# Swapping the operands of the state read, moving its scaling behind the product, and a new list of pieces

## The chip, the cores and the metric

The kernel runs on one core of one Trainium2 chip. TensorE (PE) multiplies, VectorE (DVE), ScalarE (ACT) and GpSimd (POOL) do the elementwise work, and SyncE (SP), ACT and POOL issue DMAs. The metric is the time of one execution on the device in microseconds. Before the change the median of three runs is 211.62 us (211.5 to 211.73). The profiled execution took 211.45 us in all; its span, from the first to the last instruction, is 209.7 us, so 1.75 us lie around the span, and it stands 0.17 us below the median.

## The reference

Inputs are `x` (8 batches, 8 heads, 512 rows, 64 columns) and `state` (8, 8, 32, 64), in float32. Attention is done twice, once from `x` to `state` and once from `state` to `x`:

```
scores  = x @ state.T / 8 ;  a  = softmax(scores)  ; xread = a  @ state    # 512 rows a head
scores2 = state @ x.T / 8 ;  a2 = softmax(scores2) ; sread = a2 @ x        # 32 rows a head
y = concat([xread, sread]), heads side by side: (8 * 544, 512)
out = (s * relu(y @ w_in)**2 + b) @ w_out                                  # d_ff = 2048
```

The change concerns `sread`, the second attention, whose 8 * 8 * 32 rows are computed from the softmax over the 512 rows of `x`.

## The kernel before, in words

All work is cut into small pieces. Each piece is a Python function, and a list written out by hand, `ORDER` (L15), gives the sequence in which they are emitted. A word such as `l.3.5` or `S.2.1.0.V` is a piece, its numbers and, where it can run on several engines, the engine (`A`, `V` or `G` for ACT, DVE and POOL). Each engine, and each engine's DMA queue, works strictly in the order in which its own instructions stand in the list; between engines only data and buffers make one wait for another. The first number of a word is the batch as a rule.

For one batch `b` the pieces are these. `x` or `xn` loads the rows of x (POOL's queue), `xT` or `xt` transposes them (DVE for batches 0 to 2, a DMA transpose on SP's queue for 3 to 7). `T` computes the scores into two PSUM banks; `U`, `mu`, `D`, `E1`, `z`, `At`, `A` are the first softmax. `M` multiplies the states into `w_in` (PE) and `Mc` copies that to SBUF (ACT or DVE): for `xread` the reading of the state and the first layer are one product. `l` is a block of layer 1, two matmuls of 512 columns and a Relu on ACT, through a pool of two PSUM banks (`ps_h`); `lh` is its half for the start. `s` and `sh` square it. Layer 2 is `L` with `out` for batch 0, and for batches 1 to 7 a fast form with seven products, `P.b.0` to `P.b.13`, with sums of the operands before (`S`, DVE or POOL), `ev` behind (DVE, out of PSUM) and `put` (two stores each on SP's queue). `wsum` makes the sums of weights.

The second attention: `nm`, `nms` take the maximum, `E2` is the exponential on ACT (L425), one instruction for each group of four heads, which also adds up each row. `a2` (L433) divides: a reciprocal, then two DVE instructions of 128x512 that scale and reorder. `tr` (L446) transposes by DMA on SP's queue. `V` (L450) is the product: the 64 columns of one head of x are the loaded weights and 32 columns of the transposed softmax move through, 32 matmuls a batch. `srd` (L470) copies the result on ACT straight into `srdT`, in which the batches lie side by side in the innermost place, 16 bytes from one element to the next. When all eight batches are there, `lsr`, `ssr`, `S_sr`, `P_sr` and `ev_sr` put the 2048 rows of `sread` through both layers, among the products of batches 6 and 7. `idle` are matmuls without use at the start. `cs` copies transposed states within SBUF (four DMAs on SP's queue). PSUM has two pairs of banks for `T`, `M`, `V` and others (`own` chooses), two banks for `l`, two for the products.

Of the kernel before, what the change touches and what calls it, by code (L numbers as in the profile page):

```python
# [10 lines left out]
FP32 = mybir.dt.float32  # L11
FP16 = mybir.dt.float16
# [70 lines left out]
def kernel(  # L83
# [31 lines left out]
    XB = 3  # L115
    scale = float(1.0 / np.sqrt(D))
# [59 lines left out]
    srdT = konst.tile([P, NK, Ns, B], FP16, name="srdT")  # L176
# [145 lines left out]
    def at_T(b, own=1, p=None):  # L322

        if b >= XB:
            at[b]["T", None] = T = two_banks(f"T_{b}", own=own)
            for g in range(NG):
                for c in range(2):
                    rows = slice(D * c, D * c + D)
                    for hp in range(4):
                        r = hp ^ 2 * g  # L330
                        h = 4 * g + r
                        mm(
                            T[Ns * hp : Ns * hp + Ns, c, HALF * g : HALF * g + HALF],
                            stC[rows, b - XB, g, Ns * r : Ns * r + Ns],
                            at[b]["xT"][rows, 2 * h : 2 * h + 2],
                            tp=(D * c, Ns * hp),
                        )
            return
# [131 lines left out]
    def at_srd(b):  # L470
        nc.scalar.copy(srdT[:, :, :, b], at[b]["vps"])
# [347 lines left out]
```

## Time and profile before

| | before |
|---|---|
| median of 3 runs | 211.62 us |
| profiled execution, its own time | 211.45 us |
| its span | 209.7 us |
| mean granted TensorE clock | 0.984 |
| busy: PE, DVE, ACT, POOL | 200.1, 179.0, 169.1, 47.4 us |
| chain that ended last | PE 86%, DVE 6%, DMA 3% |
| HBM read and written | 20.48 MB, 8.91 MB |

The page's first part gives each engine's busy time; its second cuts the span into 40 slices of 5.24 us and gives the busy share of each in tenths. The chain of work that ended last goes back from the last instruction, at each step to what released it. The groups of instructions give the mean duration of one and what ended the idle time before it. A view by windows gives the busy time of each engine in any stretch.

### The profile page before, as it was taken

How to read it: one execution, taken by the hardware profiler on the slowest of the kernel's cores; microseconds unless marked ns; L12 is line 12 of the kernel's file. 1: busy time of each engine (PE TensorE's matmuls, PEld its weight loads, DVE VectorE, ACT ScalarE, POOL GpSimd, SP SyncE). 2: the span in 40 equal slices, each digit the busy share in tenths (PEclk: the TensorE clock that was granted, in tenths of full speed). 3: DMA queues.
4: the chain of work that ended last, by engine and by line, in shares of the span. 5: the costliest groups of instructions: out<-in, count | busy, mean ns of one | idle time of the engine just before them, and what ended most of it. 6: DMA issues, size and time to landing. Idle time of an engine off the chain costs nothing.

```text
span 209.7 us, 4807 instructions
## 1 busy us (share of the span) xinstructions
PE 200.1 (95%) x1939; PEld 131.4 (63%) x1939; DVE 179.0 (85%) x276; ACT 169.1 (81%) x275; POOL 47.4 (23%) x63
## 2 busy tenths in 40 slices
PE   7498998999999999999999999999999999999992
PEld 2134343344576757676677677766777677888881
DVE  2998999799999899999999999999995984476571
ACT  4589999999999999989999677997989688634500
POOL 8553360524074009300470007100000000000000
PEclk9859999999999999999999999999999999999999
DMA  6999999699448539959799353719004910440055
GB/s 152 179 207 207 195 205 204 110 144 165 99 79 96 107 78 183 147 86 195 163 128 189 74 118 65 100 42 199 12 0 88 187 31 0 96 107 0 5 149 152
DMA packets 42475, 24.87 MB, mean 119 GB/s; under 512 B 24532, under 2 KB 37588, under 8 KB 42452
## 3 DMA queue, kind: packets, MB, share of 16 engines
q0 software_dynamic: 15408, 9.90, 34.0%
q1 hardware_dynamic: 25760, 13.70, 31.3%
q10 hardware_dynamic: 1284, 0.95, 1.6%
q8 instruction: 15, 0.25, 0.5%
q14 instruction: 8, 0.07, 0.1%
HBM read 20.48 MB, written 8.91 MB: 140 GB/s over the span
## 4 chain that ended last, share of the span: by engine, by line
PE 86%; DVE 6%; DMA 3%; ACT 1%; POOL 1%; issue 1%; DVEq 0%; POOLq 0%
PE opf_X L142 24%; PE hps L509 23%; PE opf_W L142 12%; PE opf_Y L142 6%; PE ops L558 5%; PE mps L142 4%; DMA w_in<-in_moe_w_in_dram 3%; PE hps_sr L509 3%; PE vps L142 2%; PE ops_sr_X L142 2%; DVE M L157 1%; PE hph L142 1%; ACT M L157 1%; PE dps L733 1%; PE ops_sr_W L142 1%; DVE g L519 1%
## 5 line engine op out<-in xcount | busy, mean ns | idle before, releaser
L513 ACT ACTIVATE r<-hps 128x512 f16<-128x512 f32 x120 | 69.2, 619 | 11.1 <-PE hps L509 9.0
L142 PEld LDWEIGHTS <-g 128*128 128x128 f16 x672 | 65.2, 98 | 17.8 <-issue 1.5
L509 PE MATMUL hps<-A,M 128*128 128x512 f16 x240 | 64.8, 379 | 0.4 <-ACT M L157 0.3
L517 ACT ACTIVATE g<-r 128x1024 f16<-128x1024 f16 (+1 forms) x37 | 46.1, 1262 | 0.0
L509 PEld LDWEIGHTS <-M 128*128 128x128 f16 x240 | 22.0, 98 | 19.7 <-issue 5.2
L142 PE MATMUL opf_X<-w_T,g 128*128 128x256 f16 x224 | 28.4, 273 | 0.0
L634 DVE TENSOR_TENSOR g<-g 128x1024 f16<-128x1024 f16 (+1 forms) x36 | 25.5, 709 | 0.6
L157 ACT CAST M<-mps 128x1024 f16<-128x1024 f32 x21 | 21.2, 1032 | 2.5 <-PE mps L142 2.5
L196 POOL DMA_DIRECT2D xn<-in_x_dram x32 | 18.5, 584 | 4.2 <-DMA w_in<-in_moe_w_in_dram 1.8
L634 POOL TENSOR_TENSOR g<-g 128x1024 f16<-128x1024 f16 x4 | 8.5, 2125 | 46.1 <-DVE g L634 32.4
L664 DVE SCALAR_TENSOR_TENSOR osx<-opf_X,sb_bc,bias_bc 128x512 f32<-128x512 f32 x21 | 15.5, 737 | 1.5 <-PE opf_X L142 1.4
L558 PE MATMUL ops<-w_out,g 128*128 128x512 f16 x64 | 16.0, 379 | 0.0
L142 PE MATMUL opf_X<-w_out,g 128*128 128x256 f16 x112 | 14.4, 273 | 0.0
L142 PE MATMUL opf_Y<-w_out,g 128*128 128x256 f16 x112 | 14.3, 273 | 0.0
L142 PE MATMUL opf_W<-w_T,g 128*128 128x256 f16 x112 | 14.2, 273 | 0.0
L142 PE MATMUL opf_X<-w_T,S 128*128 128x256 f16 x112 | 14.2, 272 | 0.0
L142 PE MATMUL opf_W<-w_out,g 128*128 128x256 f16 x112 | 13.9, 273 | 0.0
L142 PE MATMUL mps<-w_in,stT 64*32 64x512 f16 x256 | 12.4, 411 | 1.4 <-DMA w_in<-in_moe_w_in_dram 1.4
L157 DVE CAST M<-mps 128x1024 f16<-128x1024 f32 x11 | 13.2, 1215 | 0.4 <-PE mps L142 0.4
L513 ACT ACTIVATE r_sr<-hps_sr 128x256 f16<-128x256 f32 x16 | 6.1, 382 | 9.2 <-PE hps_sr L509 8.5
L142 PEld LDWEIGHTS <-S 128*128 128x128 f16 x112 | 11.0, 98 | 2.9 <-issue 0.2
L634 DVE TENSOR_TENSOR S<-g 128x1024 f16<-128x1024 f16 x14 | 9.5, 682 | 2.3 <-ACT g L517 2.2
(98 smaller groups left out, 272.9 us busy)
## 6 DMA issues: line engine op xcount, KB each, us to landing
out_dram<-osx SPq DMA_DIRECT2D x52, 128.0 KB, 2.4
xn<-in_x_dram POOLq DMA_DIRECT2D x32, 128.0 KB, 5.3
w_in<-in_moe_w_in_dram POOLq DMA_DIRECT2D x8, 256.0 KB, 9.4
w_out<-in_moe_w_out_dram POOLq DMA_DIRECT2D x4, 512.0 KB, 13.2
xh<-in_x_dram POOLq DMA_DIRECT2D x4, 256.0 KB, 11.3
out_dram<-osb SPq DMA_DIRECT2D x16, 64.0 KB, 1.8
xf<-in_x_dram SPq DMA_DIRECT2D x2, 256.0 KB, 3.6
out_dram<-osx ACTq DMA_DIRECT2D x4, 128.0 KB, 2.9
```

Source lines behind the costliest of these rows:

```text
L142: return nc.tensor.matmul(out, lhsT, rhs, start=start, stop=stop, tile_position=tp, is_transpose=is_transpose, skip_group_check=skip,)
L157: (engine.copy if engine is nc.scalar else engine.tensor_copy)(out, in_)
L196: nc.gpsimd.dma_start(out=xn_t[b][32 * jh : 32 * jh + 32].rearrange("t h c d -> t h (c d)"), in_=x[b].rearrange("h (t jh c) d -> jh t h (c ...
L509: nc.tensor.matmul(to, lhsT, rhs, start=(i == 0), stop=(i == len(terms) - 1))
L513: nc.scalar.activation(R_t[tag, q][:, i], hps, AF.Relu)
L517: nc.scalar.activation(g, r, AF.Square)
L519: e.tensor_mul(g, r, r)
L558: nc.tensor.matmul(ops_t[tag, rr], G_t[tag][:, f, P * rr : P * rr + P], w_out_f(f), start=(v == 1 and f == 4 * q), stop=(v == NKF // 4 and ...
L634: e.tensor_tensor(out, x, y, op)
L664: nc.vector.scalar_tensor_tensor(out, fast(b, name[0]), s_bc, out if plus else bias, ALU.mult, ALU.add)
L733: nc.tensor.matmul(dps, ones16[:, :P], ones16, start=True, stop=True)
```

## The change

- `V` is turned round: 32 columns of the transposed exponentials are loaded as weights, and the 64 columns of x move. The result has the rows of the state in the partitions and the columns of four heads in the free dimension. There are 32 matmuls a batch as before, now over four groups of columns of the array rather than two. With `own` 2 its place in PSUM is a bank of layer 1's pool.
- The exponentials aren't divided before the product. `a2` is gone; `E2` writes its values in the order that `a2` had written (two buffers now, one before), `tr` transposes them, and only the reciprocal, `q`, is left of the division.
- `srd` scales the product by `q` on its way out of PSUM, on ACT: one instruction of 128x64 for each group of heads, or two of 64x64 where the heads are turned (group 1 of batches 0 to 2).
- `srt`, new, transposes that 128x128 block by DMA on SP's queue, one for each batch. `sro`, new, two pieces on ACT, each of 128x512, reads the eight blocks at a step of 256 bytes and writes what `lsr` reads.
- For batches 3 to 7 the heads of group 1 aren't turned any more in `T` and `M`.
- `ORDER` is new throughout. Beside the places, engines change: of eight elementwise pieces on POOL two stay (`At.3.G`, `S.1.2.0.G`); one goes to ACT (`s.0.8.2`) and five to DVE (`D.2`, `S.1.1.1`, `S.2.2.0`, `At.5`, `S.4.4.1`). Three casts `Mc` more on ACT and three fewer on DVE, five wide squares (`s.b.f.4`, 128x2048) from ACT to DVE and one back, `castx.1` and two `turn` on DVE. In the loads, `win.1` stands before `win.0`, and `win.3` and `st` before the first `wout`.

```diff
     def at_E2(b, g):
-        E2, rs = sm(b, "E2", [P, NG, S], FP16), sm(b, "rs", [P, NG], FP32)
+        E2, rs = sm(b, "E2", [P, NG, S], FP16, bufs=2), sm(b, "rs", [P, NG], FP32)
+        if b < XB:
+            to = E2[:, g].rearrange("p (c jh t) -> p jh c t", c=4, jh=4)
+            by = scores(b)[:, g].rearrange("p (jh c t) -> p jh c t", c=4, jh=4)
+        else:
+            to = E2[:, g].rearrange("p (k c q) -> p c k q", k=2, c=2)
+            by = of_head(b, scores(b), g).rearrange("p c (k q) -> p c k q", k=2)
         nc.scalar.activation(
-            E2[:, g] if b < XB else E2[:, g].rearrange("p (c q) -> p c q", c=2),
-            of_head(b, scores(b), g), AF.Exp,
+            to, by, AF.Exp,
...
-    def at_a2(b):
-        q, a2 = sm(b, "q", [P, NG], FP32), sm(b, "a2", [P, NG, S], FP16)
-        nc.vector.reciprocal(q, at[b]["rs"])
-        for g in range(NG):
...
-            nc.vector.tensor_scalar(to, by, q[:, g : g + 1], None, ALU.mult)
+    def at_q(b):
+        nc.vector.reciprocal(sm(b, "q", [P, NG], FP32, bufs=3), at[b]["rs"])
...
     def at_V(own, *bs):
...
-                    for g in range(NG):
-                        hp = k ^ 2 * g
+                    for hp in range(4):
                         mm(
-                            vps[D * g : D * g + D, k, :],
-                            xn[:, 4 * g + k, i, :],
-                            a2T[:, SCH * g + i, Ns * hp : Ns * hp + Ns],
+                            vps[Ns * hp : Ns * hp + Ns, D * g : D * g + D],
+                            E2T[:, SCH * g + i, Ns * hp : Ns * hp + Ns],
+                            xn[:, 4 * g + (hp ^ turned(b, g)), i, :],
...
-                            tp=(0, D * g),
+                            tp=(0, Ns * hp),
...
-    def at_srd(b):
-        nc.scalar.copy(srdT[:, :, :, b], at[b]["vps"])
+    def at_srd(b, e):
+        sr16 = sm(b, "sr16", [P, P], FP16, apool, SRB)
+        for g in range(NG):
+            cols, n = slice(D * g, D * g + D), P // 2 if turned(b, g) else P
+            for p in range(0, P, n):
...
+                    nc.scalar.activation(to, by, AF.Copy, scale=q)
...
+    def at_srt(b):
+        nc.sync.dma_start_transpose(out=srdT[:, b : b + 1, :], in_=at[b]["sr16"])
...
+    def order_sr(h, e):
...
+        ks = slice(2 * h, 2 * h + 2)
+        copy(e, by_slot[0][:, ks], srdT.rearrange("p b (k n) -> p k n b", n=Ns)[:, ks])
```

The list itself is too long to show; the stretches of the new one on which the prediction rests are these, word for word, and "..." stands for what lies between:

```
l.2.5 E2.3.1 ev.1.X1 L.0.3.1 D.3.V xt.4 L.0.3.2 l.2.7 l.2.10 E1.3 T.4.0 M.2.3.1 out.0.3 wsum.T2.1.V Mc.2.3.A
nm.4 nms.4.A E2.4.1 q.3 s.2.6.2.V l.2.3 P.1.2 z.3 E2.4.0 s.2.4.2.A P.1.3 At.3.G P.1.5 M.3.0.1 P.1.4 cs.6.8
ev.1.Y l.2.13 U.4 l.2.12 P.1.7 mu.4 P.1.6 Mc.3.0.A s.2.0.2.A l.2.9 tr.3 ev.1.X2 S.1.4.1.V V.0.3 srd.3.A
...
l.6.2 P.4.11 put.3.1.0 S.5.3.0.V put.3.1.1 ev.4.X3 l.5.14 l.6.3 Mc.6.3.A s.5.14.2.A P.4.12 s.5.12.2.V P.4.13
l.6.1 P.5.3 ev.4.W2 D.7.V srt.4 M.6.1.1 M.7.1.0 Mc.7.1.A ev.4.X4 E2.7.0 S.5.1.0.V l.6.0 tr.0 q.0 l.6.8
S.5.3.1.V P.5.1 P.5.0 put.4.0.1 put.4.0.0 P.5.2 Mc.6.1.V S.5.1.1.V srt.2 E2.7.1 nm.1 q.7 E1.7 l.6.10 tr.6
S.5.2.1.V ev.5.X1 M.7.2.0 put.4.1.0 V.1.6.0 ev.5.Y l.6.11 tr.7
...
P.5.12 l.7.3 ev.5.W2 Mc.7.3.A P.6.1 l.7.7 srd.1.A put.5.0.0 put.5.0.1 s.6.4.4.V l.7.0 S.6.3.0.V srt.5 S.6.1.0.V
S.6.2.1.V P.6.0 ev.5.X4 P.6.2 l.7.15 l.7.6 srt.1 s.7.6.2.A P.6.3 s.7.2.2.V s.7.4.2.A ev.6.X1 S.6.2.0.V srt.7
l.7.9 sro.1.A l.7.11 P.6.5 put.5.1.1 ev.6.Y P.6.4 P.6.6 sro.0.A l.7.13 P.6.7 S.6.4.0.V ev.6.X2 l.7.14 s.7.0.2.A
S.6.4.1.V lsr.6
```

More of the change, by code (lines that the diff above doesn't have):

```diff
@@ L115 @@
     XB = 3
+    SRB = 4
     scale = float(1.0 / np.sqrt(D))
@@ L175 @@
     bias_bc = konst.tile([P, DM], FP32, name="bias_bc")
-    srdT = konst.tile([P, NK, Ns, B], FP16, name="srdT")
+    srdT = konst.tile([P, B, P], FP16, name="srdT")
     w_in16 = [wpool.tile([P, NK, 512], FP16, name=f"w_in16_{j}") for j in range(NJ)]
@@ L328, in at_T @@
                     rows = slice(D * c, D * c + D)
-                    for hp in range(4):
-                        r = hp ^ 2 * g
-                        h = 4 * g + r
+                    for r in range(4):
+                        hp, h = r, 4 * g + r
                         mm(
@@ L427, in at_E2 @@
         nc.scalar.activation(
-            E2[:, g] if b < XB else E2[:, g].rearrange("p (c q) -> p c q", c=2),
-            of_head(b, scores(b), g), AF.Exp,
+            to, by, AF.Exp,
             bias=at[b]["nms"][:, g : g + 1], scale=scale, accum_out=rs[:, g : g + 1],
         )
-    def at_a2(b):
-        q, a2 = sm(b, "q", [P, NG], FP32), sm(b, "a2", [P, NG, S], FP16)
-        nc.vector.reciprocal(q, at[b]["rs"])
-        for g in range(NG):
-            to, by = a2[:, g], at[b]["E2"][:, g]
-            if b < XB:
-                to = to.rearrange("p (c jh t) -> p jh c t", c=4, jh=4)
-                by = by.rearrange("p (jh c t) -> p jh c t", c=4, jh=4)
-            else:
-                to = to.rearrange("p (k c q) -> p c k q", k=2, c=2)
-                by = by.rearrange("p (c k q) -> p c k q", k=2, c=2)
-            nc.vector.tensor_scalar(to, by, q[:, g : g + 1], None, ALU.mult)
+    def at_q(b):
+        nc.vector.reciprocal(sm(b, "q", [P, NG], FP32, bufs=3), at[b]["rs"])
@@ L446, in at_tr, with turned @@
     def at_tr(b):
-        a2T = sm(b, "a2T", [P, NG * SCH, P], FP16, apool, 2)
-        nc.sync.dma_start_transpose(out=a2T, in_=at[b]["a2"].rearrange("p g s -> p (g s)"))
+        E2T = sm(b, "E2T", [P, NG * SCH, P], FP16, apool, 2)
+        nc.sync.dma_start_transpose(out=E2T, in_=at[b]["E2"].rearrange("p g s -> p (g s)"))
+    def turned(b, g):
+        return 2 * g if b < XB else 0
     def at_V(own, *bs):
-        pair = two_banks(f"vps_{bs[0]}", own=own)
+        if own == 2:
+            place = ps_h.tile([P, 512], FP32, name=f"vps_{bs[0]}", tag="ph")
+        else:
+            place = two_banks(f"vps_{bs[0]}", own=own)[:, 0, :]
@@ L453, in at_V @@
         for v, b in enumerate(bs):
-            vps = pair[:, v, : NK * Ns].rearrange("p (k n) -> p k n", n=Ns)
-            a2T, xn = at[b]["a2T"], xn_t[b]
-            for k in range(NK):
+            vps = place[:, P * v : P * v + P]
+            E2T, xn = at[b]["E2T"], xn_t[b]
+            for g in range(NG):
                 for i in range(SCH):
-                    for g in range(NG):
-                        hp = k ^ 2 * g
-                        mm(
-                            vps[D * g : D * g + D, k, :],
-                            xn[:, 4 * g + k, i, :],
-                            a2T[:, SCH * g + i, Ns * hp : Ns * hp + Ns],
+                    for hp in range(4):
+                        mm(
+                            vps[Ns * hp : Ns * hp + Ns, D * g : D * g + D],
+                            E2T[:, SCH * g + i, Ns * hp : Ns * hp + Ns],
+                            xn[:, 4 * g + (hp ^ turned(b, g)), i, :],
@@ L464, in at_V @@
                             start=(i == 0),
                             stop=(i == SCH - 1),
-                            tp=(0, D * g),
+                            tp=(0, Ns * hp),
                         )
             at[b]["vps"] = vps
-    def at_srd(b):
-        nc.scalar.copy(srdT[:, :, :, b], at[b]["vps"])
+    def at_srd(b, e):
+        sr16 = sm(b, "sr16", [P, P], FP16, apool, SRB)
+        for g in range(NG):
+            cols, n = slice(D * g, D * g + D), P // 2 if turned(b, g) else P
+            for p in range(0, P, n):
+                to, by = sr16[P - n - p : P - p, cols], at[b]["vps"][p : p + n, cols]
+                q = at[b]["q"][p : p + n, g : g + 1]
+                if e is nc.scalar:
+                    nc.scalar.activation(to, by, AF.Copy, scale=q)
+                else:
+                    e.tensor_scalar(to, by, q, None, ALU.mult)
@@ L473, in at_M @@
+    def at_srt(b):
+        nc.sync.dma_start_transpose(out=srdT[:, b : b + 1, :], in_=at[b]["sr16"])
+    by_slot = []
+    def order_sr(h, e):
+        if not by_slot:
+            by_slot.append(konst.tile([P, 2, NK, Ns, B], FP16, name="srp", tag="Ts_2")[:, 0])
+        ks = slice(2 * h, 2 * h + 2)
+        copy(e, by_slot[0][:, ks], srdT.rearrange("p b (k n) -> p k n b", n=Ns)[:, ks])
     def at_M(b, j, own):
@@ L477, in at_M @@
             for g in range(NG):
-                r = hp ^ 2 * g
+                r = hp ^ turned(b, g)
                 mm(
@@ L507, in layer1 @@
         for i, (lhsT, rhs) in enumerate(terms):
-            to = hps if len(rhs.shape) == 2 else hps.rearrange("p (c q) -> p c q", c=2)
+            to = hps if len(rhs.shape) == 2 else hps.rearrange("p (c q) -> p c q", c=rhs.shape[1])
             nc.tensor.matmul(to, lhsT, rhs, start=(i == 0), stop=(i == len(terms) - 1))
@@ L544, in layer1_sr @@
     def layer1_sr(f):
-        layer1("sr", f, [(w_in_f(k, f), srdT[:, k].rearrange("p n b -> p (n b)")) for k in range(NK)], B * Ns)
+        layer1("sr", f, [(w_in_f(k, f), by_slot[0][:, k].rearrange("p n b -> p (n b)")) for k in range(NK)], B * Ns)
     ops_t, visits = {}, {}
@@ L777 @@
         "sb": spread_scalars, "xT": at_xT, "xt": at_xt, "cs": copy_states, "T": at_T, "keep": at_keep, "U": at_U, "mu": at_mu, "D": at_D,
-        "E1": at_E1, "z": at_z, "At": at_At, "A": at_A, "nm": at_nm, "nms": at_nms, "E2": at_E2, "a2": at_a2,
-        "tr": at_tr, "V": at_V, "srd": at_srd, "M": at_M, "Mc": at_Mc,
+        "E1": at_E1, "z": at_z, "At": at_At, "A": at_A, "nm": at_nm, "nms": at_nms, "E2": at_E2, "q": at_q,
+        "tr": at_tr, "V": at_V, "srd": at_srd, "srt": at_srt, "sro": order_sr, "M": at_M, "Mc": at_Mc,
         "lh": layer1_half, "sh": square_half, "l": layer1_x, "s": square, "lsr": layer1_sr,
```

127 rows, old and new, of the table ORDER are left out of this document.

## The prediction

> **What bounds the kernel now.** I read the page's busy times and slices first.
>
> ```profile
> PE 200.1 (95%) x1939; PEld 131.4 (63%) x1939; DVE 179.0 (85%) x276; ACT 169.1 (81%) x275; POOL 47.4 (23%) x63
> PE   7498998999999999999999999999999999999992
> DVE  2998999799999899999999999999995984476571
> PEclk9859999999999999999999999999999999999999
> ```
>
> A busy PE needn't be PE at its peak, so the chain that ended last comes next, in order of time; then windows over its parts (columns: PE, PEld, DVE, ACT, POOL busy).
>
> ```profile
> 19.62 1.25 DVE U L361
> ...
> 31.34 1.25 DVE xT L311
> 32.64 0.64 PE T_None L142 x16
> 33.49 0.54 PE hps L509 x2
> ...
> 38.57 0.86 PE ops L558 x4
> ...
> 73.52 0.56 PE mps L142 x16
> ...
> 75.97 0.87 PE opf_X L142 x8
> ...
> 204.77 0.89 PE ops_sr_X L142 x8
> ```
>
> ```profile
> 33.49:83.00 49.51, 49.51 (x445) 28.16 (x443) 47.19 (x66) 48.17 (x74) 16.53 (x17) 1.00 0.72 122
> 120.00:165.00 45.00, 45.00 (x449) 31.74 (x448) 41.47 (x66) 39.03 (x64) 4.38 (x5) 1.00 0.45 85
> 165.00:205.66 40.66, 40.65 (x407) 34.20 (x404) 26.52 (x45) 21.55 (x41) 0.00 (x0) 1.00 0.29 67
> ```
>
> From 33.49 to 205.66 us the chain is PE without a gap, at full granted clock, and at the full pace: four matmuls of 512 columns in 0.86. So an `l` is 0.43 of PE's time, a `P` (8 of 256) 0.87, an `M` (8 of the 16) 0.28. Ahead of 33.49 it runs through DVE: the last link is `xT.2`, for which `T.2.1` waits. So the time is (when `T.2.1` can start) + (PE's work behind it, 172.2) + (a tail that stays). Behind 33.49 a gain can come only from less PE work; a loss from anything that makes PE wait. DVE has 49.51 - 47.19 = 2.3 us of idle time up to 83 us, 3.5 from 120 to 165. It is the engine with the least to spare.
>
> **The change, part by part.** The sum goes against the profiled execution, 211.45 us in all, 0.17 below the median of 211.62.
>
> *The product `V`.* From the chain, and one row of the groups of tile vps:
>
> ```profile
> 36.62 0.98 PE cps L142 x16
> 47.43 0.34 PE T L142 x16
> 65.51 0.61 PE vps L142 x32
> 105.13 1.16 PE vps L142 x64
> ```
>
> Before: 0.61 + 0.61 for the two single batches and 1.16 or less for each pair, 4.6 us for eight, some 18 ns a matmul. After: 32 matmuls a batch again, of 32 weight columns and 64 moving ones, in four column groups. The floor is streaming: `cps`, four groups of full height, does 16 * 512 columns in 0.98, so 32 * 64 are a quarter, 0.24. The other end is today's pace, 18 ns a matmul, 0.58. `T` loads 32-column weights and takes 0.34 for 16, with twice the moving columns a group; 13 to 14 ns, a little under today's, is nearest in kind: 0.44 a batch. **V: -1.1 us** (0 to -2.7). It stands on the chain, so all of it counts.
>
> The Trainium skill, TensorE: Matmul & The Clock Gate, section "Wait — 56ns, not 53.3ns?", says that matmuls never start less than about 25 ns apart, however few columns move. By that, 32 take 0.80 us and V costs 1.8 us more than before instead of less. The trace speaks against it for products in column groups: 64 in 1.16 us are 18 ns each.
>
> *Scaling and copies off PE.*
>
> ```profile
> L444 DVE TENSOR_SCALAR a<-E,q 128x512 f16<-128x512 f16 x16 | 4.9, 350 | 0.3
> L471 ACT CAST srdT<-vps 128x128 f16<-128x128 f32 x8 | 5.9, 740 | 0.0
> L513 ACT ACTIVATE r<-hps 128x512 f16<-128x512 f32 x120 | 69.2, 619 | 11.1 <-PE hps L509 9.0 <-DVE g L519 1.4
> L513 ACT ACTIVATE r_sr<-hps_sr 128x256 f16<-128x256 f32 x16 | 6.1, 382 | 9.2 <-PE hps_sr L509 8.5 <-DVE g_sr L519 0.4
> L517 ACT ACTIVATE g<-rh 128x512 f16<-128x512 f16 x2 | 1.3, 630 | 0.0
> L157 DVE CAST M<-mps 128x1024 f16<-128x1024 f32 x11 | 13.2, 1215 | 0.4 <-PE mps L142 0.4
> L519 DVE TENSOR_TENSOR g<-r 128x2048 f16<-128x2048 f16 x2 | 2.4, 1218 | 0.5 <-ACT r L513 0.5
> L369 DVE TENSOR_TENSOR Dm<-U,mu 128x1024 f32<-128x1024 f32 x6 | 7.3, 1210 | 0.0
> L634 DVE TENSOR_TENSOR g<-g 128x1024 f16<-128x1024 f16 x34 | 23.1, 679 | 0.6
> ```
>
> DVE loses 16 scalings, 5.6 us. ACT's `srd` changes from 8 * 0.74 = 5.9 to 5 * 2 + 3 * 3 = 19 copies of 64 columns; from 0.382 and 0.619 for 256 and 512 columns a column is 0.93 ns, so 0.20 each, 3.9. `sro` adds two of 128x512: 0.63 each if a read at a step of 256 bytes costs nothing. If it costs what the scattered write of `srdT` costs (0.74 where 0.26 would do for 128, so 3.7 ns an element more), 2.5 each. I take 0.63: a read is not that write; 2.5 is kept for the range. `E2` writes runs of 32 or 128 values, and I cost its new order at nothing; ACT's spare time before `V` would cover it.
>
> The Trainium skill, SBUF — State Buffer, section "Door 1: The DMA port swizzle", says that SBUF has lines of 16 bytes and each access to a new line pays. By that `sro` is the slow case. The 0.74 of `srdT`, one element in each 16 bytes, agrees; no row here reads so.
>
> *DVE's load.* The new list gives back what `a2` freed. Up to `P.2.0` DVE loses 4 scalings (1.4), one cast (1.2), three squares and a wide one (2.0 + 1.2) and three halves `sh` (1.2), together 7.0; it gains `D.2` (1.2) and `S.1.1.1` (0.7) from POOL, two casts (2.4), two squares and three wide ones (1.4 + 3.7), `castx.1` and two `turn` (about 1.1, estimated from the copies), together 10.5: 3.5 us more, and 4.8 with two sums and an eviction that now stand ahead of `P.2.0`. Against that it no longer meets POOL's square at the start:
>
> ```profile
> L519 DVE TENSOR_TENSOR g<-rh x6: 382/404/1328, 16.4 to 29.4; 128x512 f16<-128x512 f16 x6
> 28.08 2.33 POOL L519 TENSOR_TENSOR g<-r 128x1024 f16<-128x1024 f16 x1
> 29.36 1.33 DVE L519 TENSOR_TENSOR g<-rh 128x512 f16<-128x512 f16 x1
> ```
>
> That half square took 1.33 where its like take 0.40, and ended just behind POOL's: 0.95 saved. Net +2.5 to +3.8 us, against 2.3 of idle time up to 83. Up to `T.2.1` I walked DVE's list with these durations: `U.1` at 18.8 (19.62 before), then `Mc.0.2`, `mu`, `D`, `Mc.0.3`, a square, `turn`, `z`, `At`, `A`, `pair`, `Mc.2.0`, a half square, `xT.2`, ending at 32.8 against 32.6, with PE's work ahead of `T.2.1` equal (20 us by the pieces). **Start: +0.2** (-1 to +1.5). Behind it DVE is nearly without idle time up to 83 us, and PE needs its sums and evictions: **+0.6** (0 to 2).
>
> *SP's queue.* The transposes of DMA are now the last link of three chains.
>
> ```profile
> 52.69 4.27 SPq L572 DMA_DIRECT2D out_dram<-osb  x8
> 58.57 2.59 SPq L275 DMA_DIRECT2D stC<-stT  x4
> 139.28 2.48 SPq L673 DMA_DIRECT2D out_dram<-osx  x4
> L448 SPq DMA_TRANSPOSE a2T<-a x8: 1236/1254/1360, 57.3 to 163.3; - x8
> a2T<-a SPq DMA_TRANSPOSE x8, 3.1
> L664 DVE SCALAR_TENSOR_TENSOR osx<-opf_W,sb_bc,osx 128x512 f32<-128x512 f32 x7 | 5.2, 746 | 2.3 <-PE opf_W L142 2.3
> ```
>
> `tr.3` now stands behind `out.0.3` (4 stores) and `cs.6.8` on SP, where before `cs.6.8` came after. From the start of `out.0.3`: 0.74 on DVE, 2.1 for its stores, 2.6 for `cs.6.8`, 3.1 to landing: 8.6 us. PE's work between these places is 4 `l`, 6 `P` and an `M`: 7.2. `V.0.3` waits up to 1.4, less if DVE takes `out.0.3` early, for which 1.4 us of PE's work leaves room. I take 0.6. `tr.6` stands behind `put.4.0.1`, `put.4.0.0` (four stores, which wait for `ev.4.W2`) and `srt.2`. From the start of `ev.4.W2`: 0.74 + 2.5 + `srt.2` (0 to 1.25; the trace has no transpose that small) + 3.1 = 6.3 to 7.6. PE's work to `V.1.6.0`: 3 `l`, 3 `P`, 3 `M`, 4.7. It waits up to 2.8; nothing if DVE is 2 to 3 us ahead of the list there, where it has idle time. I take 0.6. PE waits in order, so all that stands behind `V` waits too, and ACT's `E2.1` needs the buffer that `tr.6` reads. **SP: +1.2** (0 to 4.1).
>
> Of the eight `srt` six are early; the last two aren't. SP holds `put.5.0.0`, `put.5.0.1` ahead of them, which end some 1.9 us behind the start of `srd.1` (`ev.5.W2` starts one `P` and one `l`, 1.3, ahead of it: 0.74 + 2.5 - 1.3); then `srt.5`, `srt.1` (1.25 each at most), `srt.7` (3.1 at most to landing), two `sro` and a Relu between (1.9): at most 9.4 us, against 7 `l` and 7 `P`, 9.1, up to `lsr.6`. ACT waits at `sro.1`, PE hardly: **+0.1** (0 to 4 with slow reads, when `lsr.6` and the Relus behind `sro` are late).
>
> ```profile
> 20.00:30.00 10.00, 9.63 (x65) 3.94 (x65) 9.86 (x11) 9.74 (x17) 5.00 (x6) 1.00 1.36 201
> ```
>
> The loads: `wout.0` comes behind `win.3` (0.5 MB as written) and `st` (0.2 MB), at 201 GB/s some 3.5 us later. Its first user, `L.0.0.0`, moves back by as much (three us of PE's work by the pieces). Costed at nothing; if the cover failed, the difference, 0.5. The heads no longer turned leave the number of matmuls as it is.
>
> **Sum:** 211.45 - 1.1 + 0.2 + 0.6 + 1.2 + 0.1 = **212.45**; against the median, 212.6.
>
> **Rivals.** *The waits don't come; V's gain stays (faster).* `out.0.3` runs 1.3 us ahead of its place in the list and `ev.4.W2` 2 to 3 ahead. For it: before, the chain has no DMA behind 33.49, and DVE has 3.5 us idle around `ev.4.W2`. Against: up to 83 us DVE has gained work. Then 211.45 - 1.1 + 0 = 210.4; it decides at the point where both transposes land before `V`.
>
> *`sro` is slow.* Two of 2.5, on ACT, with the Relus of the last `l` behind them: `lsr.6` some 2 late (transposes of 0.6 rather than 1.25), 214.5 with the forecast's other terms. For it: `srdT`'s write. Against: PE's 9.1 us ahead of `lsr.6`, and ACT's idle time behind 165 (21.55 busy of 40.66).
>
> *PE's floor of a matmul holds for V too.* +1.8 instead of -1.1: 215.3 with the waits, 213.4 without. Against: 18 ns measured.
>
> *It does nothing:* V at today's pace, small waits, 211.6.
>
> **How the numbers follow.** Forecast (waits of 0.8 to 3 us) 0.40; no waits 0.33; slow `sro` 0.11; PE's floor 0.04; nothing 0.12. This measurement can tell about 0.2% (0.4 us) from no change. Faster: 0.33 and a little of the last, 0.34. Same: 0.11. Slower: 0.55. The forecast's own range is 211.9 to 214; with the faster rival and its spread (V at the floor, 2.7 less) 210.1, and up to 214.6 for a slow `sro`.
>
> **What would show it.** V: `vps` at 0.4 to 0.5 us a batch in the chain; at 0.58 no gain, at 0.8 the floor. Start: `T.2.1` near 33 us. DVE: its idle time from 33 to 83 under 1.5 us, and waits of PE for `g`, `S` or `osx`. SP: PE's waits for the DMA into `E2T` before `V.0.3` and `V.1.6.0`; none of them means the faster rival. `sro`: duration of its two copies, and ACT's wait for `srdT`. I'd be wrong if `T.2.1` comes more than 1 us earlier, which the walk doesn't show, or if PE stays without gaps.

## The result and the profile after

The changed kernel is slower than the one before. In the first series it took 213.24 us (213.04 to 213.82, 4 runs) against 211.56 (211.48 to 211.73, 4 runs), a ratio of 1.0083 with a 95% interval of 1.0061 to 1.0104. A second series gave 212.14 (12 runs) against 211.44 (23 runs), 1.0035 with 1.0018 to 1.0052. The sign is the same, the size is not: 0.7 to 1.7 us. The profiled execution took 213.04 us (span 211.2), against 211.45 for the profile before.

The page's first part and its slices, after the change:

```profile
PE 197.2 (93%) x1939; PEld 129.2 (61%) x1939; DVE 179.8 (85%) x268; ACT 167.0 (79%) x286; POOL 35.1 (17%) x57
PE   4498799999999999999999989999899998999992
DVE  4798989999999989999999999988998653398671
PEclk9999999999999999999999999999999999999999
```

PE is busy 2.9 us less, and yet the span is 1.5 us longer: so PE waits. The slices with an 8 for PE in the second half of the row say where to look, and the windows (columns as in the prediction: PE, PEld, DVE, ACT, POOL busy) say how much:

```profile
33.90:83.00 49.10, 49.10 (x455) 27.90 (x456) 47.68 (x63) 45.86 (x75) 11.99 (x16) 1.00 0.89 143
120.00:165.00 45.00, 43.76 (x502) 29.96 (x500) 41.55 (x61) 37.73 (x70) 0.00 (x0) 1.00 0.40 81
165.00:207.20 42.20, 41.32 (x357) 34.64 (x355) 26.24 (x45) 23.42 (x44) 0.00 (x0) 1.00 0.25 62
```

Up to 83 us PE still has no gap; behind 120 it sits idle for 1.24 + 0.88 us, where it had 0 + 0.01 before (the ends of matmuls are modelled, so the starts, used below, say a little more). PE's list of waits behind 34 us names who it waited for (columns: us in total, times, longest):

```profile
PE hps L531 <- ACT r L535: 1.2, 2, 0.7
PE hps_sr L531 <- ACT r L535: 0.9, 1, 0.9
PE T_None L144 <- DVE xT L313: 0.3, 1, 0.3
```

No DMA and no sum of DVE is in it: apart from the start it is ACT alone, three times. ACT's timeline at those three places (start, duration, instruction, and in brackets what it was idle for):

```profile
121.77 0.59 ACT L535 ACTIVATE r<-hps 128x512 f16<-128x512 f32 x1
122.25 0.96 ACT L480 ACTIVATE sr<-vps,q 128x64 f16<-128x64 f32 x3
123.23 0.60 ACT L535 ACTIVATE r<-hps 128x512 f16<-128x512 f32 x1
...
147.75 0.95 ACT L480 ACTIVATE sr<-vps,q 128x64 f16<-128x64 f32 x3
148.72 1.06 ACT L539 ACTIVATE g<-r 128x1024 f16<-128x1024 f16 x1
149.80 0.60 ACT L535 ACTIVATE r<-hps 128x512 f16<-128x512 f32 x1
...
172.06 1.10 ACT L159 COPY srp<-srdT 128x512 f16<-128x512 f16 x1 [0.58 <-DMA out_dram<-osx]
173.07 0.58 ACT L535 ACTIVATE r<-hps 128x512 f16<-128x512 f32 x1
173.56 1.05 ACT L159 COPY srp<-srdT 128x512 f16<-128x512 f16 x1
174.51 1.08 ACT L535 ACTIVATE r<-hps 128x512 f16<-128x512 f32 x2
```

A layer-1 block needs one of two PSUM banks, which a Relu (L535) frees. At 122.25 the three copies of `srd.2` stand between two Relus, at 147.75 those of `srd.0` and a square behind them, and at 172 and 173.6 the two `sro`. The bracket names a store on SP's queue; `sro.1` reads no store's data, but what the transposes on the same queue write, and I read it as those: the last of them, issued at 167.8, took 4.1 us to land. On PE the same moments are gaps:

```profile
123.88 0.59 PE L531 MATMUL hps<-A,M 128*128 128x512 f16 x2 [0.56 <-ACT r L535]
...
150.45 0.59 PE L531 MATMUL hps<-A,M 128*128 128x512 f16 x2 [0.68 <-ACT r L535]
...
175.16 0.60 PE L531 MATMUL hps_sr<-srp,w_in 128*128 128x256 f16 x4 [0.86 <-ACT r L535]
```

From the start of each block to the next, beyond the 0.43 that a block takes, they cost 0.72 (before `l.5.7`), 0.85 (before `l.6.15`) and 1.02 (before `lsr.6`). The start and the product `V`, in the timelines of DVE and PE:

```profile
31.14 1.22 DVE L159 CAST M<-mps 128x1024 f16<-128x1024 f32 x1
32.28 0.41 DVE L541 TENSOR_TENSOR g<-rh 128x512 f16<-128x512 f16 x1
32.61 1.24 DVE L313 STREAM_TRANSPOSE xT<-xh 128x1024 f32<-128x1024 f32 x1
```

```profile
33.90 0.64 PE L144 MATMUL T_None<-xT,stZ 64*32 64x512 f16 x16 [0.25 <-DVE xT L313]
...
67.00 0.42 PE L144 MATMUL vps<-xn,E2T 128*32 128x64 f16 x32
67.35 0.41 PE L144 MATMUL mps<-w_in,stT 64*32 64x512 f16 x8
```

`T.2.1` starts at 33.90 instead of 32.64 (+1.26). `V` takes 0.35 to the start of the next product; eight batches take 2.72 instead of 4.59 (-1.87). The balance of the two profiled executions, taken at the start of the last product (206.14 against 204.61, +1.53): +1.26 - 1.87 + 0.72 + 0.85 + 1.02 = +1.98. That is 0.45 more than was measured, and I can't put the difference down to any piece. The balance names gaps; what each is worth is for the experiments to say.

### The profile page after: what moved, and what is told of

Its sections match the earlier page's. It is cut to its first block, busy times and chain, and to the rows that moved or that the text cites. A ratio compares the mean times of both kernels' runs of the same rounds, so it can differ in the third digit from the quotient of the medians.

```text
span 211.2 us, 4822 instructions
## 1 busy us (share of the span) xinstructions
PE 197.2 (93%) x1939; PEld 129.2 (61%) x1939; DVE 179.8 (85%) x268; ACT 167.0 (79%) x286; POOL 35.1 (17%) x57
## 5 line engine op out<-in xcount | busy, mean ns | idle before, releaser
L535 ACT ACTIVATE r<-hps 128x512 f16<-128x512 f32 x120 | 68.2, 605 | 12.1 <-PE hps L531 10.9
L144 PEld LDWEIGHTS <-g 128*128 128x128 f16 x672 | 65.2, 98 | 18.6 <-issue 0.9
L531 PE MATMUL hps<-A,M 128*128 128x512 f16 x240 | 65.5, 379 | 1.8 <-ACT r L535 1.2
L539 ACT ACTIVATE g<-r 128x1024 f16<-128x1024 f16 (+1 forms) x33 | 38.3, 1169 | 0.1
L656 DVE TENSOR_TENSOR g<-g 128x1024 f16<-128x1024 f16 (+1 forms) x39 | 27.7, 710 | 3.0 <-PE opf_X L144 2.5
L159 ACT CAST M<-mps 128x1024 f16<-128x1024 f32 x24 | 24.3, 1026 | 1.0 <-PE mps L144 1.0
L541 DVE TENSOR_TENSOR g<-r 128x1024 f16<-128x1024 f16 (+1 forms) x17 | 14.7, 865 | 0.4 <-ACT r L535 0.4
L535 ACT ACTIVATE r_sr<-hps_sr 128x256 f16<-128x256 f32 x16 | 6.0, 381 | 7.4 <-PE hps_sr L531 7.0
L580 PEld LDWEIGHTS <-g 128*128 128x128 f16 x64 | 6.1, 98 | 7.6 <-issue 0.7
```

The lines of the kernel that those rows point to most:

```text
L144: return nc.tensor.matmul(out, lhsT, rhs, start=start, stop=stop, tile_position=tp, is_transpose=is_transpose, skip_group_check=skip,)
L159: (engine.copy if engine is nc.scalar else engine.tensor_copy)(out, in_)
L531: nc.tensor.matmul(to, lhsT, rhs, start=(i == 0), stop=(i == len(terms) - 1))
L535: nc.scalar.activation(R_t[tag, q][:, i], hps, AF.Relu)
L539: nc.scalar.activation(g, r, AF.Square)
L541: e.tensor_mul(g, r, r)
```

## The experiments

One experiment changes a function, one nothing; all others are new lists. Their lists stand in fewer, longer lines, so that the line numbers of their profiles are 55 lower than those of the changed kernel.

**The two `srd` out of the Relus' way.**

```diff
-l.5.10 P.3.11 l.5.11 ev.3.W2 ... P.4.1 l.5.3 srd.2.A S.4.2.1.V P.4.0 ev.4.X1 l.5.9
+l.5.10 P.3.11 l.5.11 srd.2.A ev.3.W2 ... P.4.1 l.5.3 S.4.2.1.V P.4.0 ev.4.X1 l.5.9
-S.5.2.0.V srd.0.A P.5.5 s.6.0.2.A l.6.13 ... P.5.7 s.6.14.2.A P.5.9
+S.5.2.0.V P.5.5 s.6.0.2.A l.6.13 ... P.5.7 s.6.14.2.A srd.0.A P.5.9
```

> Only two words of the new list move: the copies of batch 2's and batch 0's state read on ACT go behind Relus that PE waits for (srd.2 from between l.5.3 and l.5.9 to behind l.5.11's square stretch, srd.0 from ahead of l.6.13 to behind the square s.6.14.2). Theory: the three copies of 0.32 us each hold up a Relu, and PE with it: the two gaps of 0.72 at 123.9 us and 0.85 at 150.5 us go, and the time is about 211.7 (1.5 less). Rival: PE meets the same wait one or two blocks later, since ACT has the same work in the stretch: the gaps only move, and the time is no lower than 212.9.

211.55 us (12 runs; ratio to the kernel before 0.999, 0.9965 to 1.0014). The work of ACT is the same, only its order isn't, and PE's list of waits behind 34 us has lost the row of the layer-1 blocks:

```profile
PE hps_sr L476 <- ACT r L480: 0.9, 1, 0.9
PE T_None L89 <- DVE xT L258: 0.3, 1, 0.3
```

The traces say what it was worth: from the start of `V.0.3` to that of the last product there were 139.14 and 139.23 us in the two profiles of the changed kernel, and there are 137.90 here (67.18 to 205.08). So 1.2 to 1.3 of the 1.57 us of the two gaps were won, and some 0.3 given back. The gap before `lsr.6` is still there, 1.01 by the starts.

**The last transposes ahead of four stores.**

```diff
-l.7.7 srd.1.A put.5.0.0 put.5.0.1 ... S.6.3.0.V srt.5 ... l.7.6 srt.1 ... S.6.2.0.V srt.7 l.7.9 sro.1.A
+l.7.7 srd.1.A srt.5 srt.7 put.5.0.0 put.5.0.1 ... S.6.3.0.V ... l.7.6 srt.1 ... S.6.2.0.V l.7.9 sro.1.A
```

> Only two words of the new list move: the DMA transposes srt.5 and srt.7 go ahead of the stores put.5.0.0 and put.5.0.1 on SP's queue; srt.1 stays, since it waits for the copy that ends at 166.7. Theory: sro waits for the last transposes, which stood behind 2.5 us of stores and each other; sro.1 then starts 0.7 us earlier (171.4 rather than 172.06), the gap of 1.02 before lsr.6 shrinks to 0.3 to 0.5, and the time is about 212.7 (0.5 less). Rival: srt.1 alone sets the landing, or the two sro on ACT at 1.08 us do: the time stays at 213.1 or above.

212.46 us (12 runs; 1.0037, 1.0011 to 1.0063). By the time alone this isn't faster than the second series of the changed kernel (1.0035). The gap before `lsr.6` shrank from 1.02 to 0.41, as expected, and from `V.0.3` to the last product there are 138.40 us rather than 139.14. This profile shows one more thing, PE's wait before `V.0.3`:

```profile
PE hps L476 <- ACT r L480: 1.3, 2, 0.7
PE vps L89 <- DMA E2T<-E: 1.0, 1, 1.0
PE hps_sr L476 <- ACT r L480: 0.3, 1, 0.3
```

In this execution `T.2.1` happened to start at 33.19, with the start of the list unaltered; with that same start the profiles of six executions give 33.19 to 34.08. PE came early to `V.0.3`, and `tr.3`, issued at 63.05, had not landed; it took 4.3 us where it took 3.2 in the changed kernel.

**The old start.** The list of the kernel before as far as `s.0.8.2`, and the rest of the new one.

```diff
-... l.1.12 T.2.1 l.1.3 l.1.2 L.0.1.2 s.0.14.2.A ...                             (new list)
+... l.1.12 l.1.3 T.2.1 s.0.14.2.A M.2.0.0 Mc.2.0.V s.0.8.2.G cs.3.6 l.1.13 ...  (old up to s.0.8.2.G, then new)
```

> The list of the kernel before up to its first use of T.2.1 and the square behind it (s.0.8.2 on POOL again), then the rest of the new list. Theory: the start and the rest add up, and 1.26 us of the loss is the later T.2.1 (33.90 instead of 32.64). Then T.2.1 starts at 32.6 and the time is about 212.0, 1.2 below the 213.24 of the changed kernel, still 0.4 above the kernel before. Rival: DVE carries the new list's larger load behind T.2.1 and PE waits there for sums instead: T.2.1 at 32.6 all the same, but the time no lower than 212.9.

213.06 us (12 runs; 1.0067, 1.0043 to 1.0091): the time is the rival's. PE's timeline shows the earlier start and a wait soon behind it, and the window (the third pair is DVE) that DVE has nothing left:

```profile
32.93 0.65 PE L89 MATMUL T_None<-xT,stZ 64*32 64x512 f16 x16 [0.74 <-DVE xT L258]
...
36.45 0.59 PE L476 MATMUL hps<-A,M 128*128 128x512 f16 x2 [0.39 <-ACT r L480]
```

```profile
34.00:66.20 32.20, 31.66 (x248) 16.25 (x247) 31.99 (x40) 29.31 (x50) 7.59 (x9) 1.00 0.75 128
```

The same window of the changed kernel, and of the kernel before:

```profile
34.00:66.20 32.20, 32.20 (x267) 16.64 (x264) 31.75 (x40) 30.39 (x54) 8.43 (x10) 1.00 0.80 134
```

```profile
34.00:66.20 32.20, 32.20 (x290) 16.92 (x287) 30.57 (x42) 31.77 (x51) 12.56 (x12) 1.00 0.74 123
```

DVE is busy 31.75 of 32.20 us in the new list and 30.57 in the old one. Of the 0.97 us by which `T.2.1` came earlier nothing is left: `V.0.3` starts at 67.12 instead of 67.00. The waits that PE shows on the way aren't for DVE's sums, as the rival had it. By the starts, 0.56 was lost at the block at 36.45, whose bank was freed by a Relu behind the square `s.0.12.2` on ACT, and 0.28 at the product at 40.40 that reads `c`, which DVE made late; 0.34 is an `M` that the old start leaves behind `T.2.1`. What ties the far end to DVE is the queue of SP, on which `tr.3` stands behind the stores of `out.0.3`:

```profile
58.49 0.74 DVE L590 SCALAR_TENSOR_TENSOR osb<-ops,sb_bc,bias_bc 128x512 f32<-128x512 f32 x1
```

In the changed kernel DVE starts `out.0.3` at 58.49, and `V.0.3` follows 8.51 behind it. Here the two are at 58.76 and 67.12, 8.36 apart, and the transpose lands 0.05 before `V.0.3`. By this, an earlier start counts only as far as DVE comes earlier to `out.0.3`.

**All three.**

```diff
+l.1.3 T.2.1 s.0.14.2.A M.2.0.0 Mc.2.0.V s.0.8.2.G ... l.5.11 srd.2.A ... s.6.14.2.A srd.0.A ... srd.1.A srt.5 srt.7 put.5.0.0
```

> The three edits together: the start of the kernel before, the two srd behind the Relus, srt.5 and srt.7 ahead of the stores. Theory: the losses add, since PE has no other gap: 213.24 less 1.26, 1.5 and 0.5 is about 210.0, faster than the kernel before by 1.6, which is about what V gained on PE (1.87). Rival: they are one slack that another engine gives back: 211.5 or above.

211.47 us (12 runs; 0.9986, 0.9963 to 1.0009): 1.6 less than with the old start alone, and no better than the two `srd` alone. The losses don't add with the old start, as the rival said, and the next kernel does without it.

**The two that gained, and the changed kernel again** (unaltered).

```diff
+l.5.11 srd.2.A ... s.6.14.2.A srd.0.A ... srd.1.A srt.5 srt.7 put.5.0.0
```

> The changed kernel once more, unaltered, so that the other kernels of this series have it on the same chip: 213.2, and T.2.1 between 33.2 and 34.1, the spread that the three profiles with this start have shown.

> The two edits that gained alone, together and without the old start: the two srd behind the Relus, and srt.5 and srt.7 ahead of the stores. Theory: their losses lie in different places and add: 213.24 less 1.7 and 0.8 is 210.8 (210.4 to 211.2), faster than the kernel before. Rival: the one hides the other: 211.5 or above.

212.14 us for the changed kernel (12 runs) and 210.61 for the two edits (12 runs; 0.9969, 0.9947 to 0.9991), on the same chip: 1.5 us, and faster than the kernel before. From `V.0.3` to the last product there are 137.12 us rather than 139.23. PE's waits behind 34 us are down to one row:

```profile
PE hps_sr L476 <- ACT r L480: 0.2, 1, 0.2
```

**The strided read of `sro`.**

```diff
-copy(e, by_slot[0][:, ks], srdT.rearrange("p b (k n) -> p k n b", n=Ns)[:, ks])
+copy(e, by_slot[0][:, ks].rearrange("p k n b -> p (k n b)"),
+     srdT.rearrange("p (h b) m -> p h (b m)", h=2)[:, h])
```

> The changed kernel, but sro reads its two halves of srdT one element behind the other instead of at a step of 256 bytes, so the rows of sread go in a wrong order and the last rows of the output aren't the reference's. Theory that the step costs time: the two copies take 0.62 each, as other copies of 128x512 in SBUF do, rather than 1.05 to 1.10. Rival: the size or ACT's start sets the 1.08: they stay above 0.95.

The rows of the state's attention then come in a wrong order, so this kernel serves for the durations alone. 211.93 us in its one run, which says nothing by itself. The groups, with the changed kernel's in the second fence:

```profile
L104 ACT COPY srp<-srdT 128x512 f16<-128x512 f16 x2 | 1.2, 613 | 0.1
```

```profile
L159 ACT COPY srp<-srdT 128x512 f16<-128x512 f16 x2 | 2.2, 1076 | 0.6 <-DMA out_dram<-osx 0.6
```

The step costs ACT 0.46 us a copy, 0.93 for both, and without it PE has no wait before `lsr.6` at all. The list is that of the changed kernel. So taking away either of the two, the late transposes (0.41 of the gap left) or the slow read (nothing left), closes most of it.

**The new operations with the old list.** `q` where `a2` was, `srd` at its old place, `srt` and `sro` added, `lsr.14` and `lsr.10` a few products later.

```diff
-... tr.1 s.7.0.2.A ... srd.7 ... V.1.1 ... srd.1 ... P.6.10 s.7.6.2.A put.5.1.1 lsr.14 s.7.8.2.A P.6.11 P.6.13 lsr.10 P.6.12
+... tr.1 srt.6 s.7.0.2.A ... srd.7.A srt.7 ... V.1.1 ... srd.1.A srt.1 ... P.6.10 s.7.6.2.A put.5.1.1 s.7.8.2.A P.6.11 P.6.13
+s.7.10.2.A sro.1.A sro.0.A P.6.12 lsr.14 lsr.10
```

> The kernel's functions of the change with the list of the kernel before: q where a2 was, srd on ACT at its old place, the eight srt behind existing DMA words, sro.1 and sro.0 behind the square s.7.10.2 and lsr.14, lsr.10, lsr.15 three products later. Theory: the new list cost the time and not the new operations: PE has V's 1.9 less to do, DVE 5.6 us less, no place on the old list loses more than 0.4, and the time is 209.4 to 210.4, below the kernel before. Rival: the new operations cost it themselves (transposes that land late, copies on ACT between Relus): 211.5 or above, with PE waiting for E2T, or for srp at lsr.14.

217.96 us (6 runs; 1.0277, 1.0242 to 1.0312). SP issues in order, and a small transpose that waits for its `srd` holds what stands behind it. SP's timeline at the end, and the wait that came of it:

```profile
167.86 8.01 SPq L430 DMA_TRANSPOSE srdT<-sr  x3
175.96 14.19 SPq L640 DMA_DIRECT2D out_dram<-osx  x12
```

```profile
DVE osx L631 <- DMA out_dram<-osx: 6.5, 1, 6.5
PE opf_W L89 <- DVE osx L631: 3.5, 1, 3.5
```

The stores of batch 5 come behind `srt.1`, DVE can't evict into the buffer that they read, and PE waits 3.5 us for a PSUM bank. Earlier, `srt.4` stood ahead of `xt.6` and waited for `srd.4`; PE lost 1.8 before `T.6.1`. That was where I had put the words, not the operations themselves, so both were moved:

```diff
-tr.5 srt.4 ... xt.6      ->  +tr.5 ... xt.6 srt.4
-tr.1 srt.6 ... srt.1 ... put.5.1.1 ... put.5.1.0  ->  +tr.1 put.5.1.1 put.5.1.0 srt.6 ... srt.1
```

> The new operations with the old list again, without the two places where a small transpose, waiting on SP for its srd, held up what stands behind it: srt.4 goes behind xt.6, and put.5.1.1 and put.5.1.0 ahead of srt.6, srt.7 and srt.1. Theory: the 1.8 us that PE lost before T.6.1 and the 3.7 before P.6.10 go, and V's 1.9 less remains, with 0.6 lost to srd.1 between Relus: about 210.2 (209.5 to 210.8), below the kernel before. Rival: the chain V.1.1, srd.1, srt.1, sro, lsr.14 is too long for the old list's end by itself: 211.5 or above, with PE waiting at lsr.14.

212.50 us (12 runs; 1.0051, 1.0034 to 1.0068). Both places are free of waits now, and `P.6.0` starts at 160.58 where it started at 161.37 before the change; then the end takes it back:

```profile
PE hps_sr L476 <- ACT srp L104: 1.0, 1, 1.0
```

`lsr.14` waits for `sro`, which ACT starts at 178.45, right behind three squares; that place was my choice. So the old list doesn't hold the longer chain (`V.1.1`, `srd.1`, `srt.1`, `sro`) as it stands; whether a better place for the squares would have been enough wasn't tried.

**DVE relieved by POOL.** All three edits, with `s.0.8.2` on DVE, `D.2` and `S.1.1.1` on POOL, `s.0.12.2` a Relu later, and `c` ahead of a sum.

```diff
-xT.2 ... s.0.8.2.G ... s.0.12.2.A wsum.T2.0.V l.1.2 ... mu.2 wsum.T1.1.V ... c ... D.2.V ... S.1.1.1.V
+xT.2 s.0.8.2.V ... wsum.T2.0.V l.1.2 s.0.12.2.A ... mu.2 c wsum.T1.1.V ... D.2.G ... S.1.1.1.G
```

> The old start with the two other edits (the kernel of 211.47), and DVE relieved ahead of V.0.3: the square s.0.8.2 on DVE instead of POOL at the start (0.65 on DVE instead of the 0.95 to 2.0 that a half square or At.1 lost beside POOL's square), D.2 and S.1.1.1 on POOL as in the kernel before (1.9 us less on DVE), s.0.12.2 between other Relus and c ahead of a sum of weights. Theory: up to V.0.3 DVE is the bound (33.2 of the 33.3 us from 33.9 to 67.1 busy), so a better start can only count if DVE has less to do: T.2.1 at about 32.1, V.0.3 by 65.7, the time about 210.0. Rival: the transposed E2T or POOL's long operations (2 us each, and DVE held up beside them) set V.0.3: it stays at 66.7 or later and the time at 211.3 or above.

217.33 us (5 runs; 1.0274, 1.0251 to 1.0298). `T.2.1` came at 31.72, and POOL spoilt it in two ways. Its timeline and DVE's, side by side:

```profile
38.03 1.91 POOL L315 TENSOR_TENSOR Dm<-U,mu 128x1024 f32<-128x1024 f32 x1 [10.07 <-DVE mu L311]
47.12 2.12 POOL L601 TENSOR_TENSOR g<-g 128x1024 f16<-128x1024 f16 x1 [7.19 <-DVE S L601]
49.19 2.30 POOL L143 DMA_DIRECT2D xn<-in_x_dram  x4
```

```profile
38.45 2.03 DVE L571 TENSOR_TENSOR w_T<-w_out 128x1024 f16<-128x1024 f16 x1
47.58 2.75 DVE L486 TENSOR_TENSOR g<-r 128x2048 f16<-128x2048 f16 x1
```

```profile
PE T L89 <- DMA xT<-xn: 4.4, 1, 4.4
```

The two instructions of DVE that met POOL's took 2.03 and 2.75 where their like take 0.67 and 1.18. They ended 0.54 and 1.09 us behind POOL's, a little less than their usual time, as if they had stood still beside it. And `xn.4` is issued on POOL behind `S.1.1.1`, so x of batch 4 came late, and PE waited 4.4 us at `T.4.0`. That second wait says nothing on the question; it was left out next.

**The same without POOL.**

```diff
-D.2.G ... S.1.1.1.G
+D.2.V ... S.1.1.1.V
```

> The kernel of 211.47 (old start, srd and srt moved) without what the join of the two lists had brought: the square s.0.8.2 on DVE instead of POOL, s.0.12.2 a Relu later, c ahead of a sum of weights; nothing goes to POOL this time. Theory that DVE is the bound from T.2.1 to V.0.3: T.2.1 comes at 31.7, but V.0.3 only at 66.0 to 66.7, the time 209.9 to 210.6. Rival, the start counts in full: V.0.3 at 64.9 and the time about 208.9.

210.69 us (9 runs; 0.9962, 0.9938 to 0.9987). `T.2.1` starts at 32.02, 1.5 earlier than in the kernel of the two edits, `V.0.3` at 66.23, 0.4 earlier. So 1.1 of the 1.5 us is lost by then, though the two waits named under the old start, at 36.45 and 40.40, are no longer there. The time is no lower than that of the two edits without the old start. DVE is full again:

```profile
34.00:66.20 32.20, 31.89 (x249) 16.23 (x247) 31.99 (x42) 30.07 (x52) 8.48 (x10) 1.00 0.78 132
```

`out.0.3` starts on DVE at 57.87 and `V.0.3` again 8.36 behind it (58.10 and 66.61 in the kernel of the two edits). That DVE sets the pace of this stretch fits both kernels with the early start; only one of PE's small waits in it is put down to DVE by name (0.2 for `osb`).

**The end and the start once more.** The two edits, `sro.0` on DVE, and two half squares out of the way.

```diff
-mu.1 D.1.V sh.0.4.1.A l.0.8 ... Mc.1.3.A      ->  +mu.1 D.1.V l.0.8 ... Mc.1.3.A sh.0.4.1.A
-cs.3.6 sh.0.2.1.V Mc.1.2.A xT.2 ... wsum.T2.0.V  ->  +cs.3.6 Mc.1.2.A xT.2 ... wsum.T2.0.V sh.0.2.1.V
-ev.6.Y P.6.4 P.6.6 sro.0.A                     ->  +ev.6.Y P.6.4 P.6.6 sro.0.V
```

> The kernel of 210.61 with three words more moved: the half squares sh.0.4.1 (ACT) and sh.0.2.1 (DVE) go out of the way of E1.1 and xT.2 at the start, and sro.0 goes to DVE, beside sro.1 on ACT. Theory: DVE's 0.54 of waiting for E1.1 ahead of z.1 goes, T.2.1 starts 0.5 to 0.9 earlier, DVE's load up to V.0.3 lets about 0.5 of it through, and the gap of 0.41 before lsr.6 goes: 209.7 (209.3 to 210.2). Rival: a start that comes earlier is given back before V.0.3, and only the 0.4 of sro counts: 210.2 or above.

210.15 us (12 runs; 0.9939, 0.9911 to 0.9967), the lowest of all and 0.6% faster than the kernel before; its interval overlaps that of the two edits (0.9947 to 0.9991). The gap before `lsr.6` is gone, and from `V.0.3` to the last product there are 136.70 us rather than 137.12; the start isn't better (`T.2.1` at 33.89, and PE no longer waits there: it comes that late itself). So the rival was right on the start. DVE takes about half of ACT's time for the same strided read:

```profile
L104 ACT COPY srp<-srdT 128x512 f16<-128x512 f16 x1 | 1.1, 1076 | 0.0
L104 DVE COPY srp<-srdT 128x512 f16<-128x512 f16 x1 | 0.6, 600 | 0.0
```

## Why the prediction was right and where it was wrong

The forecast was 212.6 us; 213.24 and 212.14 were measured, and slower was the likeliest sign. But that the sum came out was luck: its errors cancel, and the main loss was not in it.

- **V, -1.1: right in kind, too small.** 32 matmuls take 0.34 us, 10.6 ns each, not 13 to 14; eight batches gain 1.87. The Trainium skill, TensorE: Matmul & The Clock Gate, section "Wait — 56ns, not 53.3ns?", would have them at no less than about 25 ns; this case's trace contradicts that for products in four column groups. The rival with a floor under each matmul is out.
- **Scaling and copies off PE: the step that failed.** I priced `srd` at 19 times 0.20 and put it "off PE", without asking what stands behind it on ACT. It takes 0.317 each at the median, 5.6 us of ACT's time in all:

```profile
L480 ACT ACTIVATE sr<-vps,q x19: 307/317/388, 68.0 to 166.4; 128x64 f16<-128x64 f32 x13, 64x64 f16<-64x64 f32 x6
```

  Three in a row are 0.95 us between two Relus, and PE has only two banks ahead of a Relu. The two gaps on PE were 1.57 us; moving two words won 1.2 to 1.3 of them (213.24 or 212.14 to 211.55). That more banks would have hidden the copies wasn't tried.
- **`sro`, +0.1: too small.** The gap was 1.02. The rival of a slow `sro` named the right mechanism, a read that pays for its step, with a wrong price: the step costs 0.46 a copy rather than 1.9. It and the stores ahead of the last transposes make up the gap, which I had seen as closed by 9.4 against 9.1 us.
- **Start, +0.2, and DVE without idle time, +0.6: not two terms, and together too small.** My walk gave `xT.2` ending at 32.8; it ended at 33.85, and `T.2.1` came 1.26 late. PE doesn't wait for a sum behind it, but the late start isn't the cause either: an earlier `T.2.1` (32.93 for 33.90, 32.02 for 33.51) moved `V.0.3` by +0.12 and -0.4 only. `V.0.3` comes 1.56 later than before (67.00 for 65.44), of which 0.43 is one more `l` that the new list puts ahead of it. DVE has the least to spare on the whole way to `out.0.3`, wherever `T.2.1` starts; so its load, my reason for the +0.6, is the likeliest one. No kernel here takes work off DVE in this stretch without another change, so that it alone sets the other 1.1 isn't shown.
- **SP's queue, +1.2: no wait, but no slack either.** The working held: from the start of `out.0.3` on DVE at 58.49 to `V.0.3` at 67.00 are 8.5 us, where I had 8.6. DVE took `out.0.3` early enough, which I had named as the condition, and PE came just then. In the execution with `T.2.1` at 33.19 PE waited 1.0 for `E2T`. Before `V.1.6.0` there was no wait.
- **The rival without waits, 210.4**, is near what the new operations give once the orders of ACT and SP are mended: 210.61, and 210.15 with `sro.0` on DVE. In part that is luck too: the rival had 1.1 for `V` and nothing for the start, and the traces have 1.87 and, in the kernel of 210.61, a `V.0.3` that comes 1.17 later than before, 0.74 without that `l`. The sentence that PE without gaps would prove me wrong was the right test; the gaps were there, in other places.

## What to carry to other kernels

An instruction that is "off the critical engine" still stands in a queue: before costing it at nothing, read the two instructions around it on its own engine, and ask how many buffers lie between the one behind it and the engine that bounds. An early start was worth little here with DVE full behind it, so read the busy time of all engines in the stretch that follows before working on a first wait. A transfer that waited for its data held up all that stood behind it on SP's queue, so put it behind what is ready, or ahead of it only if its data is.

## What the runs showed of the hardware

- Matmuls of 32 weight columns and 64 moving ones, in four column groups, start 10.6 ns apart (32 in 0.34 us).
- On ACT, a copy of 128x512 that reads at a step of 256 bytes takes 1.08 us and 0.61 without the step; on DVE the same strided read takes 0.60. The Trainium skill, SBUF — State Buffer, section "Door 1: The DMA port swizzle", has each access to a new line of 16 bytes pay. ACT agrees in sign: 0.9 ns an element. That is under a third of what the write of `srdT` paid before, by an estimate: 128 columns should take 0.34, between the 0.33 of 64 and the 0.38 of 256 in the profile after, and took 0.74, so 3.1 ns an element. What DVE pays isn't shown, since no run has the dense copy on it; its nearest rows of that size take 0.35 (a scaling, before) and 0.42 (a copy out of PSUM).
- While POOL runs a tensor operation, two elementwise operations of DVE on float16 tensors took 2.03 and 2.75 us rather than 0.67 and 1.18.
- A DMA transpose of 128x128 takes as long as one of 128x1024, by the medians after the change: 1.24 us to issue and 3.0 to land, against 1.25 and 3.1.
- With an unaltered start, `T.2.1` began anywhere from 33.19 to 34.08 us, so a difference of less than 1 us at the start can't be read from one profile.
